# First blocks of batches 4 to 7: four turns in a row in score banks, two batches' scores in one burst, and the ban as a mask on VectorE

## Chip, cores and metric

The kernel runs on one core of one Trainium2 chip. The metric is the device time of an execution in microseconds (us). A core has TensorE (PE, with its weight loads shown as PEld), VectorE (DVE), ScalarE (ACT), GpSimd (POOL) and SyncE (SP, which here only issues transfers).

## What is computed

The reference is an attention with a forgetting gate, followed by a feed-forward layer on all 4608 rows:

```python
# q, k, v: 8 batches x 8 heads x 576 x 64; f: 8 x 8 x 576
scores = (1 / 8) * q @ k^T
cum    = cumsum(log(clip(f, 1e-4, 1)))
scores = where(causal, -1e9, scores + cum[:, :, :, None] - cum[:, :, None, :])
attn   = softmax(scores)
x      = (attn @ v) as 4608 rows of 512
h      = x @ w_in                      # 512 -> 2048
out    = (h * sigmoid(h)) @ w_out      # 2048 -> 512
```

The kernel takes the decay out of the softmax: v and a column of ones are multiplied by a weight per key, and the sums that come out in that column divide the rest.

## The kernel before

The 576 rows of a sequence are split into a first block of 128 rows, three more of 128, and a tail of 64. The **first blocks** of all eight batches are done ahead of the main loop, each with all eight heads at once. The **main loop** runs over 32 pairs of heads (n = 0 to 31), four pairs to a batch, and does the other rows. The **feed-forward** layer is work without order of its own: `m1_chunk` (lines 560 to 583) makes 128 of the 2048 hidden features for one group of rows (PE into a bank `hp`, tanh on ACT into `th`, the gate on DVE into `gt`), and `m2_part` (594 to 626) a quarter of an output tile `po`, which ACT copies and POOL stores. `fill` (698) puts such chunks between the attention's steps, by a budget in us at assumed costs, and `least` chunks in any case. So the order on each engine is fixed when the program is built; every engine runs its own list from front to back and waits for semaphores.

A first block of batch b has these steps:
- `load_qk0` (128): POOL issues the loads of q and k, as bf16, into a tile `qkb`.
- `turn0(b, i)` (277): 16 matmuls of 64x64 turn q (i = 0) or k (i = 1) into a bank `tp`; ACT copies q to `qT0` (a cast), DVE copies k to `kT0`.
- `ban0` (297): two matmuls of 512 columns put -30000 above the diagonal into a score tile, ahead of the scores. Or `mask0` (333): DVE multiplies the exponentials by a triangle of ones.
- `scores0` (309): 8 matmuls into a score tile `sc` of two banks, and one exp of 1024 columns on ACT.
- `out0` (349): 8 matmuls with the weighted v (`convert_v0`, 339, on POOL), then a reciprocal and a product on DVE into `xq`.
- `back0` (382): 4 transposes on PE into a bank `tx`, copied by ACT into the rows `x` that the feed-forward layer reads.

PSUM has eight banks: two score tiles of two banks each (pool `psc`, also for `out0`), and four single banks (pool `pbig`, tag `big`) that `tp`, `hp`, `po` and `tx` share.

Batches 0 to 3 form group 0 of the feed-forward's rows (512 wide), batches 4 and 5 group 1, 6 and 7 group 2 (256 wide each), and the main loop's rows groups 3 and on (384 wide, the tails 256). The change is in `two_more` (805), which does the first blocks of batches 4 and 5, and of 6 and 7, between chunks of the feed-forward layer: for 4 and 5 only first-layer chunks of group 0 are ready; from line 830 on the second layer is allowed too (`open2`). A group's chunks may start when `ready` has it.

In the main loop `scores(n, c)` (444) needs q and k of pair n turned: POOL casts them (`cast_qk`, 394), SP issues a transposing transfer into `qkT`, of which there are three (`transposes`, 423), SP also issues all loads, and POOL, in one list, casts, weights v (`convert_v`, 409) and issues the stores of finished output tiles.

Of the kernel before, what the change touches and what calls it, by code (L numbers as in the profile page):

```python
# [10 lines left out]
FP32 = mybir.dt.float32  # L11
BF16 = mybir.dt.bfloat16
P = 128
# [5 lines left out]
def kernel(  # L19
# [17 lines left out]
    NP = H // 2  # L37
    SM = 512
# [9 lines left out]
    RUN = 8  # L48
    NRUN = P // RUN
# [18 lines left out]
    psc = ctx.enter_context(tc.tile_pool(name="psc", bufs=2, space=bass.MemoryType.PSUM))  # L68
    pbig = ctx.enter_context(tc.tile_pool(name="pbig", bufs=4, space=bass.MemoryType.PSUM))
# [204 lines left out]
    qT0: dict[int, bass.AP] = {}  # L274
    u0: dict[int, bass.AP] = {}

    def turn0(b, i):
        src = qk0[b]
        if i == 0:
            qT0[b] = qktp.tile([P, NP, P], BF16, name="qT0", tag="qT0", bufs=2)  # L280
        dst, evac = ((qT0[b], nc.scalar.copy), (kT0[b], nc.vector.tensor_copy))[i]
        tp = pbig.tile([P, NP, NRUN, RUN], FP32, name="tp", tag="big")
        for c in range(RUN):
            for j in range(2):
                nc.tensor.matmul(
                    tp[j * D : (j + 1) * D, :, :, c].rearrange("p a r -> p (a r)"),
                    lhsT=src[:, i, c * D : (c + 1) * D],
                    rhs=sel[:, j, :],
                    start=True,
                    stop=True,  # L290
                )
        evac(
            out=dst[:, :, :].rearrange("p a t -> p (a t)"),
            in_=tp[:, :, :, :].rearrange("p a r c -> p (a r c)"),
        )

    def ban0(b):
        sc = psc.tile([P, 2, NP, P], FP32, name="sc", tag="sc")
        for i in range(2):
            nc.tensor.matmul(  # L300
                sc[:, i, :, :].rearrange("p a t -> p (a t)"),
                lhsT=ident_bf[:, :],
                rhs=ban[:, :, :].rearrange("p a t -> p (a t)"),
                start=True,
                stop=False,
            )
        return sc

    def scores0(b, sc=None):
        t = qT0.pop(b)  # L310
        fresh = sc is None
        u = upool.tile([P, 2, NP, P], BF16, name="u", tag="u")
        u0[b] = u
        if fresh:
            sc = psc.tile([P, 2, NP, P], FP32, name="sc", tag="sc")
        for p in range(NP):
            for i in range(2):
                r = slice(i * D, (i + 1) * D)
                nc.tensor.matmul(
                    sc[:, i, p, :],  # L320
                    lhsT=kT0[b][r, p, :],
                    rhs=t[r, p, :],
                    start=fresh,
                    stop=fresh or p == NP - 1,
                )
        nc.scalar.activation(
            out=u[:, :, :, :].rearrange("p i a t -> p (i a t)"),
            in_=sc[:, :, :, :].rearrange("p i a t -> p (i a t)"),
            func=ACT.Exp,
            scale=scale,  # L330
        )

    def mask0(b):
        x = u0[b][:, :, :, :].rearrange("p i a t -> p (i a) t")
        nc.vector.tensor_tensor(
            out=x, in0=x, in1=tri[:, None, :].to_broadcast([P, H, P]), op=ALU.mult
        )
# [11 lines left out]
    def out0(b, step_=2, apart=False):  # L349
        if apart:  # L350
            dns = [pbig.tile([P, 1, 4, D + 1], FP32, name="dn1", tag="big") for _ in range(2)]
        else:
            dn = psc.tile([P, 2, 4, P], FP32, name="dn0", tag="sc")
            dns = [dn[:, g : g + step_, :, :] for g in range(0, 2, step_)]
        k = 2 // len(dns)
        u = u0.pop(b)
        for h in range(H):
            p, i = h // 4 * 2 + h % 2, h // 2 % 2
            nc.tensor.matmul(
                dns[h // 4 // k][:, h // 4 % k, h % 4, 0 : D + 1],  # L360
                lhsT=u[:, i, p, :],
                rhs=v0[b][:, h, :],
                start=True,
                stop=True,
            )
        rec = recp.tile([P, 2, 4], FP32, name="rec0", tag="rec0")
        if not apart:
            nc.vector.reciprocal(out=rec[:, :, :], in_=dn[:, :, :, D])
        xq = xqp.tile([P, H, D], BF16, name="xq", tag="xq")
        for g, part in enumerate(dns):  # L370
            r = rec[:, g * k : (g + 1) * k, :]
            if apart:
                nc.vector.reciprocal(out=r, in_=part[:, :, :, D])
            nc.vector.tensor_tensor(
                out=xq[:, 4 * k * g : 4 * k * (g + 1), :].rearrange("p (g j) d -> p g j d", j=4),
                in0=part[:, :, :, 0:D],
                in1=r[:, :, :, None].to_broadcast([P, k, 4, D]),
                op=ALU.mult,
            )
        xqs[b] = xq  # L380
# [275 lines left out]
    def step(force=0):  # L656

        a, c = at["m1"], at["m2"]
        want = wanted(a, c)
        if not want:  # L660
            return None
        g1 = M1[a][0] if a < len(M1) else NG
        g2 = M2[c][0] if c < len(M2) else NG
        can1 = g1 in ready and not (M1[a][1] == 0 and g1 > g2 + 1)
        can2 = open2["w"] and c < len(M2) and g2 < g1
        kind = force if (force == 1 and can1) or (force == 2 and can2) else want
        if kind == 1:
            if M1[a][1] == 0:
                begin[g1] = (0, c)
            m1_chunk(g1, M1[a][1])  # L670
            at["m1"] += 1
            t = 4 * (GW[g1] / 2.4 + 2.5)
        else:
            m2_part(*M2[c])
            at["m2"] += 1
            t = 4 * (DM / 2.4 + 2.5)
        return t
# [6 lines left out]
    def plan(us_):  # L684

        a, c, kinds = at["m1"], at["m2"], []
        while us_ > 0:
            k = wanted(a, c)
            if not k:
                break  # L690
            kinds.append(k)
            if k == 1 and M1[a][1] == 0:
                begin[M1[a][0]] = (0, c)
            us_ -= (4 * (GW[M1[a][0]] / 2.4 + 2.5) if k == 1 else 4 * (DM / 2.4 + 2.5)) / 1000
            a, c = a + (k == 1), c + (k == 2)
        return kinds

    def fill(us_, least=0, ends=(0, 0)):

        left = us_ + at["left"]  # L700
        kinds = plan(left)
        kinds += [0] * (least - len(kinds))
        if any(ends) and kinds:
            if 2 not in kinds:
                kinds[0] = 2
            n1, n2 = len(kinds) - kinds.count(2), kinds.count(2)
            e0 = 1 if ends[0] else 0
            e1 = 1 if ends[1] and n2 > e0 else 0
            inner = n2 - e0 - e1
            n = n1 + inner  # L710
            mid = [2 if (x + 1) * inner // n > x * inner // n else 1 for x in range(n)]
            if inner and mid[-1] == 2 and e1 and not e0:
                mid = mid[::-1]
            kinds = [2] * e0 + mid + [2] * e1
        for k in kinds:
            t = step(k)
            if t is None:
                at["left"] = 0.0
                return
            left -= t / 1000  # L720
        at["left"] = left
# [3 lines left out]
    on_act, on_dve = nc.scalar.copy, nc.vector.tensor_copy  # L725
    weights_scan()
    turn0(0, 0)
    keep_warm(1)
    turn0(0, 1)
    nc.vector.tensor_copy(out=wexp[:, S : S + ST], in_=wexp[:, SM:S])  # L730
    bans = [ban0(0), ban0(1)]
# [4 lines left out]
    convert_v0(0)  # L736
    load_w_in(0)
    turn0(1, 0)
    turn0(1, 1)
    turn0(2, 0)  # L740
# [61 lines left out]
    for c in range(NM):  # L802
        convert_v(0, c)

    def two_more(b, banned):
        for x in range(2):
            turn0(b + x, 0)
            turn0(b + x, 1)
            fill(0.6, 1)
        for x in range(2):  # L810
            if banned:
                scores0(b + x, ban0(b + x))
            else:
                scores0(b + x)
                mask0(b + x)
            fill(0.6 if x == 0 else 2.0 if banned else 2.8, 1 if x == 0 else 2)
        out0(b)
        fill(0.6, 1)
        out0(b + 1)
        fill(0.8, 2)  # L820
        back0(b, on_act)
        fill(0.6, 1)
        back0(b + 1, on_act)
        fill(0.6, 1)

    fill(5.0)
    two_more(4, True)
    ready.add(1)
    fill(5.0)
    open2["w"] = True  # L830
    begin[M1[at["m1"]][0]] = (M1[at["m1"]][1], at["m2"])
    fill(6.0)
    two_more(6, False)
    ready.add(2)
    fill(3.2)

# [37 lines left out]
    for m in range(NQ):  # L874
# [5 lines left out]
        if m > 0:  # L880
            back(m - 1)
            if m % 2 == 0:
                b = m // 2 - 1
# [56 lines left out]
```

## Time and profile before

| what | us |
|---|---|
| executions: median of 3 (lowest, highest) | 343.55 (343.11, 345.07) |
| span of the profiled execution; its time isn't listed apart | 342.2 |
| PE busy | 334.3 |
| ACT, DVE, POOL busy | 216.8, 180.5, 130.0 |
| `two_more` for batches 4 and 5 | 23.4 to 36.3 |
| `two_more` for batches 6 and 7 | 46.6 to about 59.7 |
| first scores of the main loop | 61.1 |

The span reaches from the first to the last instruction that the profiler shows; the executions' times are some 1.35 us longer than it. "Busy" is the time in which an engine has an instruction in work; matmuls overlap, so a busy PE may still step slower than it could, and the distance from start to start tells more than the length of one. In a list by time each row has start, length, engine, line, operation, output and inputs, shape and count; a bracket gives the idle time ahead of it and what ended it. An operation such as `128*64 128x64` is a matmul with weights of 128 rows by 64 columns.

### The profile page before, as it was taken

How to read it: one execution, taken by the hardware profiler on the slowest of the kernel's cores; microseconds unless marked ns; L12 is line 12 of the kernel's file. 1: busy time of each engine (PE TensorE's matmuls, PEld its weight loads, DVE VectorE, ACT ScalarE, POOL GpSimd, SP SyncE). 2: the span in 40 equal slices, each digit the busy share in tenths (PEclk: the TensorE clock that was granted, in tenths of full speed). 3: DMA queues.
4: the chain of work that ended last, by engine and by line, in shares of the span. 5: the costliest groups of instructions: out<-in, count | busy, mean ns of one | idle time of the engine just before them, and what ended most of it. 6: DMA issues, size and time to landing. Idle time of an engine off the chain costs nothing.

```text
span 342.2 us, 8881 instructions
## 1 busy us (share of the span) xinstructions
PE 334.3 (98%) x3560; PEld 198.6 (58%) x3560; DVE 180.5 (53%) x387; ACT 216.8 (63%) x401; POOL 130.0 (38%) x227
## 2 busy tenths in 40 slices
PE   7999999999999999999999999999999999999995
PEld 3645655567656556566465666656656565555654
DVE  4665736357647547357445563655746364444330
ACT  5857645877687676857759677595685944454431
POOL 8895317732618307327325422612830000001011
PEclk9999999999999999999999999999999999999999
DMA  8999999999699889999999789989994010001012
GB/s 154 185 184 221 192 192 155 233 207 190 142 172 205 188 177 168 180 210 156 174 188 188 171 156 202 169 170 165 165 186 101 22 42 33 31 32 61 33 53 72
DMA packets 142457, 50.67 MB, mean 148 GB/s; under 512 B 133328, under 2 KB 139728, under 8 KB 142416
## 3 DMA queue, kind: packets, MB, share of 16 engines
q1 hardware_dynamic: 132400, 32.93, 56.7%
q0 software_dynamic: 9856, 17.04, 21.5%
q8 instruction: 28, 0.46, 0.6%
q10 hardware_dynamic: 160, 0.13, 0.1%
q14 instruction: 13, 0.11, 0.1%
HBM read 36.85 MB, written 9.44 MB: 135 GB/s over the span
## 4 chain that ended last, share of the span: by engine, by line
PE 66%; DMA 14%; SPq 9%; POOL 6%; issue 3%; ACT 0%; POOLq 0%
PE po L612 29%; PE hp L567 25%; DMA vf<-in_v_dram 6%; PE sc L459 5%; SPq L158 5%; PE dn L506 4%; DMA w_out_bf<-in_moe_w_out_dram 3%; PE dn L515 2%; SPq L427 2%; DMA qkT<-qkb 2%; POOL qkb L399 1%; DMA qkb<-in_k_dram 1%; SPq L168 1%; SPq L179 1%; DMA qf<-in_q_dram 1%
## 5 line engine op out<-in xcount | busy, mean ns | idle before, releaser
L576 DVE SCALAR_TENSOR_TENSOR gt<-th,hp 128x384 bf16<-128x384 bf16 (+2 forms) x208 | 105.8, 522 | 119.0 <-ACT th L575 115.5
L575 ACT ACTIVATE th<-hp 128x384 bf16<-128x384 f32 (+2 forms) x208 | 95.2, 478 | 84.3 <-PE hp L567 82.0
L612 PE MATMUL po<-w_out_bf,gt 128*128 128x512 bf16 (+1 forms) x592 | 145.3, 374 | 0.0
L567 PE MATMUL hp<-x,w_in_bf 128*128 128x384 bf16 (+2 forms) x704 | 128.1, 321 | 0.2
L567 PEld LDWEIGHTS <-w_in_bf 128*128 128x128 bf16 x832 | 79.9, 98 | 56.5 <-issue 0.7
L463 ACT ACTIVATE u<-sc 128x1024 bf16<-128x1024 f32 (+1 forms) x96 | 75.3, 822 | 9.5 <-PE sc L459 9.5
L612 PEld LDWEIGHTS <-gt 128*128 128x128 bf16 x592 | 53.3, 98 | 47.9 <-issue 2.5
L591 POOL DMA_DIRECT2D out_dram<-osb x38 | 21.0, 552 | 93.7 <-ACT osb L622 66.7
L413 POOL TENSOR_TENSOR vp<-vf,w_bf 128x520 bf16<-128x520 f32 (+1 forms) x32 | 34.4, 1078 | 41.0 <-DMA vf<-in_v_dram 35.1
L622 ACT ACTIVATE osb<-po 128x512 f32<-128x512 f32 (+1 forms) x37 | 22.1, 597 | 18.9 <-PE po L612 18.9
L399 POOL CAST qkb<-qf 128x384 bf16<-128x384 f32 x32 | 16.7, 521 | 41.9 <-DMA qf<-in_q_dram 41.2
L459 PE MATMUL sc<-qkT 64*128 64x128 bf16 (+1 forms) x640 | 26.9, 207 | 0.9 <-DMA qkT<-qkb 0.8
L459 PEld LDWEIGHTS <-qkT 64*128 64x128 bf16 x640 | 18.4, 94 | 12.5 <-issue 10.2
L467 ACT ACTIVATE ut<-sc 128x640 bf16<-128x640 f32 x32 | 23.3, 729 | 0.0
L476 DVE TENSOR_TENSOR u<-u,tri 128x768 bf16<-128x768 bf16 x32 | 22.1, 690 | 1.2 <-ACT u L463 1.2
L399 POOL CAST qkb<-kf 128x384 bf16<-128x384 f32 x32 | 17.7, 554 | 13.0 <-DMA kf<-in_k_dram 12.8
L506 PEld LDWEIGHTS <-u 128*128 128x128 bf16 x576 | 20.8, 98 | 2.5
L506 PE MATMUL dn<-vp,u 128*128 128x65 bf16 x384 | 21.8, 194 | 0.0
L524 DVE TENSOR_TENSOR xr<-dn,rec 128x448 bf16<-128x448 f32 x32 | 20.0, 624 | 1.1
L506 PE MATMUL dn<-v,u 128*128 128x65 bf16 x192 | 19.8, 194 | 0.0
L482 DVE TENSOR_TENSOR ut<-ut,trit 128x128 bf16<-128x128 bf16 x32 | 11.2, 351 | 15.6 <-ACT ut L467 15.6
L567 PE MATMUL hp<-xt,w_in_bf 128*128 128x256 bf16 x128 | 17.7, 273 | 0.0
(68 smaller groups left out, 203.0 us busy)
## 6 DMA issues: line engine op xcount, KB each, us to landing
out_dram<-osb POOLq DMA_DIRECT2D x32, 256.0 KB, 3.3
vf<-in_v_dram SPq DMA_DIRECT2D x26, 256.0 KB, 4.7
qf<-in_q_dram SPq DMA_DIRECT2D x64, 96.0 KB, 2.9
kf<-in_k_dram SPq DMA_DIRECT2D x64, 96.0 KB, 3.1
w_in_bf<-in_moe_w_in_dram POOLq DMA_DIRECT2D x4, 512.0 KB, 6.9
w_out_bf<-in_moe_w_out_dram POOLq DMA_DIRECT2D x4, 512.0 KB, 9.6
vf<-in_v_dram POOLq DMA_DIRECT2D x6, 256.0 KB, 10.3
qkb<-in_q_dram POOLq DMA_DIRECT2D x8, 128.0 KB, 5.1
```

The source lines that it names most:

```text
L399: nc.gpsimd.tensor_copy(out=t2[:, c0 : c0 + NR, :].rearrange("p c x -> p (c x)"), in_=t[:, :, :, :].rearrange("p c h d -> p (c h d)"),)
L413: nc.gpsimd.tensor_tensor(out=vbf[b][r, c, :, :], in0=vst[b][c][r, :, :], in1=w_bf[r, c + 1, b * H : (b + 1) * H, None].to_broadcast([n, H ...
L459: nc.tensor.matmul(sc[:, i, o : o + q1 - q0], lhsT=kt, rhs=t[r, q0:q1], start=True, stop=True)
L463: nc.scalar.activation(out=u[:, :, c * SM : c * SM + w], in_=sc[:, :, 0:w], func=ACT.Exp, scale=scale)
L467: nc.scalar.activation(out=ut[:, :, 0:3:2, :].rearrange("p k i t -> p i k t"), in_=sc[:, :, T0 : T0 + (NM + 1) * ST].rearrange("p i (k t) ...
L476: nc.vector.tensor_tensor(out=x, in0=x, in1=tri[:, None, None, :].to_broadcast([P, 2, NR, P]), op=ALU.mult)
L506: nc.tensor.matmul(dn[:, i * NR + c - 1, :], lhsT=u[:, i, o : o + P], rhs=vals(kb, i), start=(kb == 0), stop=(kb == c),)
L567: nc.tensor.matmul(hp[:, :], lhsT=w_in_bf[:, cc, fc * P : (fc + 1) * P], rhs=xcols(g, cc), start=(cc == 0), stop=(cc == NCC - 1),)
L575: nc.scalar.activation(out=th[:, :], in_=hp[:, :], func=ACT.Tanh, scale=0.5)
L576: nc.vector.scalar_tensor_tensor(out=gt[:, fc, :], in0=th[:, :], scalar=1.0, in1=hp[:, :], op0=ALU.add, op1=ALU.mult,)
L612: nc.tensor.matmul(po[:, :], lhsT=gt[:, fc, tb * P : (tb + 1) * P], rhs=w_out_bf[:, fc, m0:m1], start=(fc == 0), stop=(fc == NFC - 1),)
L622: nc.scalar.activation(out=osb[:, :], in_=po[:, :], func=ACT.Copy, scale=0.5)
```

## The change

In `two_more` the four turns of two batches come one after the other, with no chunks between them, each batch's two turns in the two banks of one score tile. The scores of both batches follow together. All four batches get the mask on DVE; the ban on PE is dropped for batches 4 and 5 (it stays for 0 to 3). The chunks between are redistributed, with budgets of 1.4 and 3.4 us in place of 0.6, 0.6, 0.6 and 2.0 (or 2.8).

```diff
-    def turn0(b, i):
+    def turn0(b, i, pair=None):
...
-        tp = pbig.tile([P, NP, NRUN, RUN], FP32, name="tp", tag="big")
+        if pair is None:
+            tp = pbig.tile([P, NP, NRUN, RUN], FP32, name="tp", tag="big")
+        else:
+            tp = pair[:, i, :].rearrange("p (a r c) -> p a r c", a=NP, c=RUN)
...
-    def two_more(b, banned):
+    def two_more(b):
         for x in range(2):
-            turn0(b + x, 0)
-            turn0(b + x, 1)
-            fill(0.6, 1)
-        for x in range(2):
-            if banned:
-                scores0(b + x, ban0(b + x))
-            else:
-                scores0(b + x)
-                mask0(b + x)
-            fill(0.6 if x == 0 else 2.0 if banned else 2.8, 1 if x == 0 else 2)
+            pair = psc.tile([P, 2, SM], FP32, name="tq", tag="sc")
+            turn0(b + x, 0, pair)
+            turn0(b + x, 1, pair)
+        fill(1.4, 2)
+        scores0(b)
+        scores0(b + 1)
+        mask0(b)
+        mask0(b + 1)
+        fill(3.4, 3)
         out0(b)
         fill(0.6, 1)
         out0(b + 1)
...
     fill(5.0)
-    two_more(4, True)
+    two_more(4)
...
-    two_more(6, False)
+    two_more(6)
```

## Prediction

> **What bounds the kernel now.** I read the page first, then what PE waited for, then PE's order of time from 20 to 112 us, then ACT, DVE and POOL in the same stretches, then the chain that ended last.
>
> ```profile
> span 342.2 us, 8881 instructions
> PE 334.3 (98%) x3560; PEld 198.6 (58%) x3560; DVE 180.5 (53%) x387; ACT 216.8 (63%) x401; POOL 130.0 (38%) x227
> ```
>
> PE has work in 98% of the span, so the time is PE's work plus its few waits. The waits are found in PE's order of time (start, length, engine, line, what, idle before):
>
> ```profile
> 73.70 0.28 PE L459 MATMUL sc<-qkT 64*128 64x64 bf16 x8
> 74.38 0.40 PE L459 MATMUL sc<-qkT 64*128 64x128 bf16 x8 [0.40 <-DMA qkT<-qkb]
> ...
> 111.07 0.28 PE L459 MATMUL sc<-qkT 64*128 64x64 bf16 x8
> 111.78 0.40 PE L459 MATMUL sc<-qkT 64*128 64x128 bf16 x8 [0.43 <-DMA qkT<-qkb]
> ```
>
> Eight such matmuls give way to the next group after about 0.12 us (0.28 less the last one's tail of some 0.17), so 74.38 comes 0.56 us late and 111.78 0.60 us late: the transposed q and k of head pairs 3 and 9 land too late. The chain that ended last says the same. Up to 111.78 it holds transfers, SP and POOL, and from there PE alone:
>
> ```profile
> 107.88 3.86 DMA qkT<-qkb
> ...
> 111.78 0.40 PE sc L459 x8
> ```
>
> So until 112 us an earlier PE meets a transfer, and after it every us of PE counts.
>
> **What goes.** PE around the first blocks of batches 4 and 5, and of 6:
>
> ```profile
> 24.45 1.04 PE L567 MATMUL hp<-x,w_in_bf 128*128 128x512 bf16 x4
> 25.42 1.08 PE L285 MATMUL tp<-sel,qkb 128*64 128x64 bf16 x32
> 26.43 1.04 PE L567 MATMUL hp<-x,w_in_bf 128*128 128x512 bf16 x4
> 27.31 0.59 PE L300 MATMUL sc<-ban,ident_bf 128*128 128x512 bf16 x2
> 27.83 0.40 PE L319 MATMUL sc<-qT,kT 64*128 64x128 bf16 x8
> 28.16 1.04 PE L567 MATMUL hp<-x,w_in_bf 128*128 128x512 bf16 x4
> ...
> 46.60 1.08 PE L285 MATMUL tp<-sel,qkb 128*64 128x64 bf16 x32
> 47.62 0.61 PE L567 MATMUL hp<-x,w_in_bf 128*128 128x256 bf16 x4
> ```
>
> Steps from start to start are the cost here, since lengths overlap. Four 512-wide matmuls step 0.88 us before the ban (26.43 to 27.31) and 0.97 before a turn (24.45 to 25.42): going into the narrow shapes costs 0.09.
> - Bans of batches 4 and 5: 27.31 to 27.83 is 0.52 us, less the 0.09 of entering the scores, which stays: 0.43. Twice: **-0.86**.
> - Scores of two batches in one burst: two bursts of 0.33 (27.83 to 28.16) and an entry of 0.09 each become one entry and 0.55 (the eight more matmuls step 0.22; leaving is paid once). -0.2 in each of two places: **-0.4**.
>
> **What the four turns in a row cost.** The built program of the changed kernel carries a wait that the diff doesn't show: the first matmul of every turn of k waits for ACT's copy of q out of the same score tile, though that copy reads the tile's other bank. Before, the turns had tiles of their own. No row of before has this wait, but its parts do:
>
> ```profile
> 47.28 0.58 ACT L292 CAST qT<-tp 128x512 bf16<-128x512 f32 x1 [1.86 <-PE tp L285]
> ```
>
> ACT starts 0.68 us after the turn pair does (46.60) and needs 0.58; with some 0.04 for the signal the turn of k starts at 1.30 instead of 0.45. The next batch's turn of q has another tile and follows at once (1.75), its turn of k starts at 3.05, and the filler at 3.62. Before, the two bursts took 1.02 each (46.60 to 47.62) and a second entry of 0.09, in all 2.13. So +1.49 a burst, in two bursts: **+2.98**. What is queued behind the wait on PE is everything, for no filler stands within the burst. Bounds: no wait at all gives -0.2 a burst; a copy that starts a whole 0.6 us ACT row later, twice a burst, gives +2.7. I take 1.49, whose parts are rows.
>
> The skill bears on this: the Trainium skill, "PSUM — Partial Sum Buffer", section "PSUM bank collisions raise a hardware error", asks for semaphores by bank and quadrant, and says that different banks don't collide. By that rule the wait isn't needed, and a program guarded so would come out as my first rival; but here the program's own wait decides.
>
> **What the masks and the long burst cost.** For batches 4 and 5 both exps and both masks now stand ahead of the filler's tanh on ACT and gate on DVE. Rows:
>
> ```profile
> 51.64 1.14 DVE L335 TENSOR_TENSOR u<-u,tri 128x1024 bf16<-128x1024 bf16 x1 [1.66 <-ACT u L326]
> 53.04 1.20 DVE L335 TENSOR_TENSOR u<-u,tri 128x1024 bf16<-128x1024 bf16 x1
> ...
> 35.35 2.00 DVE L576 SCALAR_TENSOR_TENSOR gt<-th,hp 128x512 bf16<-128x512 bf16 x3
> ```
>
> With the filler's start after the turns as zero: scores are issued by 2.38, exps end at 3.47 and 4.40 (1.02 each), masks at 4.7 and 5.8, and gates follow at 0.60 each (2.00 for three is 0.69 and 0.65 a step). Four filler banks are full at 5.84; the fifth chunk, after out0, is due at 6.10 and gets its bank at 6.39 (0.29). The DVE then has two divisions of 0.85 among the gates: the chunk after the first way back is due at 9.46 and starts at 9.63 (0.17). The last way back is issued by 10.72, and here group 0 is used up: the chunk after it is group 1's first, which reads what ACT copies out of that way back. ACT is at a tanh until 11.2, then copies until 11.77:
>
> ```profile
> 36.52 0.58 ACT L390 COPY x<-tx 128x512 bf16<-128x512 bf16 x1
> ```
>
> Before, a 512-wide chunk of group 0 stood over this copy; in the changed order none is left. PE waits 1.09. Together 1.55, against 0.45 lost before in this stretch (four 512-wide matmuls take 1.10 from 34.96 to 36.06 instead of 0.88, and the 4 of 512 and 24 of 256 columns from 36.28 to 40.02 take 3.74 where 4 x 0.216 + 24 x 0.108 are 3.46): **+1.1**, between 0 (DVE had been early) and 1.6. For batches 6 and 7 the masks were there already, and the filler is half as heavy on DVE: nothing.
>
> POOL converts v beside these masks:
>
> ```profile
> 30.02 2.11 POOL L340 TENSOR_TENSOR v<-vf,w_bf 128x520 bf16<-128x520 f32 x2 [3.98 <-DMA vf<-in_v_dram]
> ...
> 51.19 2.51 POOL L340 TENSOR_TENSOR v<-vf,w_bf 128x520 bf16<-128x520 f32 x2
> ```
>
> Two conversions took 2.11 us alone and 2.51 beside masks. In the new order they end by 32.5, and out0 of batch 4 is due at about 33: hidden.
>
> **What moves.** Counting the matmuls in both orders, the changed one has 8 more 256-wide and 8 more 512-wide filler matmuls ahead of the main loop's first scores (8 x 0.108 + 8 x 0.216 = 2.6 us); the total is the same. With -0.86 -0.4 +2.98 +1.1 = +2.8 PE reaches the first scores 5.4 us later. Then the tiles of pairs 3 and 9 have landed: **-1.16**, and the score bank that came 0.27 late at 63.2 is free: **-0.2**. SP's and POOL's orders keep loads and transposes as they were. On POOL a fourth store now stands ahead of pair 3's casts and one that PE releases at about 73.4 ahead of pair 4's (70.8 before); a transpose also waits for scores three pairs back. I estimate 1 to 2 us for these on the transfers, less than PE's own delay there. Later the filler ahead shrinks to +0.9 (pair 13) and -0.65 (pair 17): pair 13's tile landed at 139.2, 0.6 ahead of its scores, pair 17's 1.2 ahead, so a PE that is 1.5 later than before on balance still finds them, by under 2 us.
>
> **Sum.** -0.86 -0.4 +2.98 +1.1 -1.16 -0.2 = +1.46 us on a span of 342.2. The median of the runs is 343.55, 1.35 above the span; I leave this as it is: **345.0**.
>
> **Rivals.**
> 1. The turns don't wait (the copy is done when the matmul asks): bursts -0.4 instead of +2.98, so PE loses 0.6, arrives at pairs 13 and 17 earlier than they land, and gives back some 0.6 of the 1.36: 343.55 -0.6 -1.36 +0.6 = 342.2. For it: the banks differ. Against it: the built wait. 0.08.
> 2. The backlog costs nothing (DVE caught up during the turn stalls): 345.0 - 1.1 = 343.9. 0.15.
> 3. The transfers slide with PE: POOL's store ahead of pair 4's casts holds them until PE gets there, and every later load and transpose is behind them on SP, so the two waits at pairs 3 and 9 return elsewhere (9, 13 or 17): 345.0 + 1.36 = 346.4, slower. It decides once the transfers slip by over 2 us at pair 13. For it: transfers set the chain up to 112 us. Against it: between those slots SP waits for POOL some us, which is slack. 0.25.
>
> The forecast has 0.52. The range takes in rival 3 and most of rival 2: 343.6 to 346.8. About what this measurement can tell from no change is 0.5%, 1.72 us: 345.27 and 341.83. Slower by more: rival 3 and some three tenths of the forecast, 0.40; faster by more: 0.04; within: 0.56.
>
> **What would show it.** In the changed profile: a gap of about 0.85 us ahead of each of four turns of k, released by ACT's cast; a gap near 1 us after the last way back of batch 5, released by the copy; no wait for qkT at pairs 3 and 9; PE's busy time down by 1 to 2 us while its gaps grow. It is wrong if the turns run without gaps, if pairs 9, 13 or 17 wait for transfers, or if new waits on score banks appear in the main loop.

## The result, and the profile after

The changed kernel takes 347.02 us (median of 6 runs, 346.81 to 348.22), the kernel before 344.41 in the same comparison (6 runs, 343.11 to 345.74). The ratio is 1.0072, 95% interval 1.0043 to 1.0101: slower by 1.5 to 3.5 us. The forecast was +1.46 us and 345.0. Of the 2.02 us that it missed by, 0.86 is the base, whose median went from 343.55 with three runs to 344.41 with six; the other 1.16 is the change itself, +2.61 by the medians. In the runs here an execution's time lies 1.73 to 1.95 us above its own span, not 1.35, so the span of 342.2 that the sum started from stands for about 344.0 (an estimate from these).

The profiled execution of the changed kernel ran 347.17 us with a span of 345.4. The page's head and its line of engines:

```profile
span 345.4 us, 8880 instructions
...
PE 334.5 (97%) x3556; PEld 199.3 (58%) x3556; DVE 180.9 (52%) x389; ACT 217.0 (63%) x401; POOL 129.1 (37%) x227
```

PE has as much busy time as before in a span that is 3.2 us longer. So the loss is idle time of PE. What PE waited for (us in total, times, longest), from the view of waits:

```profile
PE tq L288 <- ACT qT L295: 2.7, 4, 0.7
...
PE dn L509 <- DVE gt L579: 0.9, 2, 0.5
PE hp L570 <- ACT x L393: 0.9, 1, 0.9
...
PE tx L551 <- DVE xr L527: 0.4, 1, 0.4
```

Before, from batch 4 on, PE's order of time showed two waits of this kind alone, 0.40 and 0.43 us for transfers. The first and the third line were forecast. The second and the fourth were not, and the second decides this case. PE in order of time in the first blocks of batches 4 and 5 (start, length, line, what, idle before):

```profile
23.05 0.64 PE L288 MATMUL tq<-sel,qkb 128*64 128x64 bf16 x16
24.36 1.08 PE L288 MATMUL tq<-sel,qkb 128*64 128x64 bf16 x32 [0.68 <-ACT qT L295]
26.12 0.64 PE L288 MATMUL tq<-sel,qkb 128*64 128x64 bf16 x16 [0.67 <-ACT qT L295]
26.69 0.60 PE L570 MATMUL hp<-x,w_in_bf 128*128 128x512 bf16 x2
...
38.39 0.81 PE L570 MATMUL hp<-x,w_in_bf 128*128 128x256 bf16 x6 [0.86 <-ACT x L393]
```

A group of 16 is one turn. After the turn of q at 23.05 PE stands still until ScalarE has copied q; the 32 at 24.36 are the turn of k and the next batch's turn of q, and then PE stands again. ScalarE's side of it:

```profile
23.73 0.58 ACT L295 CAST qT<-tq 128x512 bf16<-128x512 f32 x1
25.49 0.58 ACT L295 CAST qT<-tq 128x512 bf16<-128x512 f32 x1 [1.17 <-PE tq L288]
```

The copies end at 24.31 and 26.07, and the turns of k start 0.05 us later each.

A gap in brackets counts from the modelled end of the last matmul. In what follows a step is called **late** by what it takes from start to start beyond the same pair of shapes where nothing waits; the gap of 0.68 is 0.90 late, that of 0.86 is 1.02. From the first turn of batch 4 PE needs 37.64 us to the main loop's first scores before and 42.90 after (61.07 - 23.43, 65.95 - 23.05). I count from that turn, because in the profiled executions of this study it comes anywhere from 22.9 to 25.4 us, with the same code ahead of it in all of them.

The first scores of pairs 3 and 9 stand without a gap behind the 64-wide ones of the pair before them now, eight and eight in one row of 16. Pair 17's do not:

```profile
78.53 0.50 PE L462 MATMUL sc<-qkT 64*128 64x64 bf16 x16
...
116.17 0.50 PE L462 MATMUL sc<-qkT 64*128 64x64 bf16 x16
...
169.74 0.40 PE L462 MATMUL sc<-qkT 64*128 64x128 bf16 x8 [0.33 <-DMA qkT<-qkb]
```

Instead PE is late at places that had no wait before: 0.42 at 75.8 (transposes behind VectorE's division), 0.57, 0.30 and 0.62 at 83.9, 110.9 and 190.7, each at the first matmul of a pair's second attend, and 0.49 at pair 17. PE, VectorE and GpSimd around the first of these second attends, from the timeline:

```profile
82.99 1.05 POOL L416 TENSOR_TENSOR vp<-vf,w_bf 128x520 bf16<-128x520 f32 x1 [6.30 <-DMA vf<-in_v_dram]
...
83.17 0.94 DVE L485 TENSOR_TENSOR ut<-ut,trit 128x128 bf16<-128x128 bf16 x1 [0.76 <-ACT ut L470]
...
84.04 0.74 DVE L579 SCALAR_TENSOR_TENSOR gt<-th,hp 128x256 bf16<-128x256 bf16 x2
84.50 0.19 PE L509 MATMUL dn<-v,u 128*128 128x65 bf16 x1 [0.41 <-DVE gt L579]
```

Read from the bottom: the attend needs a bank of the pool "big", which the first of the two gates at 84.04 frees; that gate stands on VectorE behind the tail mask of the same pair; and the tail mask takes 0.94 us. The same mask ten us earlier:

```profile
73.08 0.22 DVE L485 TENSOR_TENSOR ut<-ut,trit 128x128 bf16<-128x128 bf16 x1 [0.74 <-ACT ut L470]
```

What is different at 83 is POOL's line: GpSimd converts v at the time. The theory from here on, **A**: the four gaps are ScalarE's copies; the gap at 38.39 is the order of chunks; and the time that the prediction thought won in the main loop goes into masks that meet conversions. The rivals are named with each run.

### The profile page after: what moved, and what is told of

It is laid out like the page before. It is cut to its first block, busy times and chain, and to the rows that moved or that the text cites. A ratio compares the mean times of both kernels' runs of the same rounds, so it can differ in the third digit from the quotient of the medians.

```text
span 345.4 us, 8880 instructions
## 1 busy us (share of the span) xinstructions
PE 334.5 (97%) x3556; PEld 199.3 (58%) x3556; DVE 180.9 (52%) x389; ACT 217.0 (63%) x401; POOL 129.1 (37%) x227
## 4 chain that ended last, share of the span: by engine, by line
PE 77%; ACT 6%; DMA 5%; SPq 4%; DVE 3%; issue 3%; POOL 1%; POOLq 0%; ACTq 0%
PE po L615 32%; PE hp L570 29%; PE sc L462 5%; PE dn L509 4%; DMA vf<-in_v_dram 3%; ACT th L578 2%; PE dn L518 2%; SPq L158 2%; DMA qkT<-qkb 2%; DVE gt L579 2%; PE wm L232 1%; ACT u L466 1%; PE tq L288 1%; ACT ut L470 1%; DVE ut L485 1%
## 5 line engine op out<-in xcount | busy, mean ns | idle before, releaser
L570 PE MATMUL hp<-x,w_in_bf 128*128 128x384 bf16 (+2 forms) x704 | 126.4, 321 | 1.0 <-ACT x L393 0.9
L416 POOL TENSOR_TENSOR vp<-vf,w_bf 128x520 bf16<-128x520 f32 (+1 forms) x32 | 35.7, 1114 | 42.5 <-DMA vf<-in_v_dram 31.4
L479 DVE TENSOR_TENSOR u<-u,tri 128x768 bf16<-128x768 bf16 x32 | 20.7, 648 | 3.1 <-ACT u L466 3.1
L402 POOL CAST qkb<-kf 128x384 bf16<-128x384 f32 x32 | 16.6, 519 | 9.5 <-DMA kf<-in_k_dram 9.5
```

The lines of the kernel that those rows point to most:

```text
L402: nc.gpsimd.tensor_copy(out=t2[:, c0 : c0 + NR, :].rearrange("p c x -> p (c x)"), in_=t[:, :, :, :].rearrange("p c h d -> p (c h d)"),)
L416: nc.gpsimd.tensor_tensor(out=vbf[b][r, c, :, :], in0=vst[b][c][r, :, :], in1=w_bf[r, c + 1, b * H : (b + 1) * H, None].to_broadcast([n, H ...
L570: nc.tensor.matmul(hp[:, :], lhsT=w_in_bf[:, cc, fc * P : (fc + 1) * P], rhs=xcols(g, cc), start=(cc == 0), stop=(cc == NCC - 1),)
```

## Experiments: the first blocks

All ratios are to the kernel before, from runs on the same chip.

**The copies after both turns.** Nothing else is changed in the changed kernel; `turn0` hands its copy back in place of issuing it.

```diff
...
-            turn0(b + x, 0, pair)
-            turn0(b + x, 1, pair)
+            copies = [turn0(b + x, i, pair) for i in range(2)]
+            for copy in copies:
+                copy()
```

> The changed kernel, but each batch's two copies (q on ACT, k on DVE) are issued after both turns, so that no turn of k waits for ACT. Theory A (the four gaps of 0.90 us ahead of the turns of k cost their full length): 3.6 us less than the changed kernel, about 0.99 us under the kernel before, with four gaps gone in PE's order and the other waits of the changed kernel unchanged. Rival B (the transfers set the pace of the main loop, and a PE that is early gives the time back there): under 1.5 us gained on the changed kernel, the rest as new waits for qkT.

344.12 us, ratio 1.0002 (0.9979 to 1.0025). The turns of a burst run as one row:

```profile
23.37 1.98 PE L288 MATMUL tq<-sel,qkb 128*64 128x64 bf16 x64
25.28 1.04 PE L575 MATMUL hp<-x,w_in_bf 128*128 128x512 bf16 x4
```

From the first turn to the main scores 39.31 us instead of 42.90: 3.59 less, four times 0.90. So the gaps are the wait for the copy and nothing else, and in size they are about the whole of the change's loss. That the kernel comes out level with the kernel before and not under it is a first sign that the main loop doesn't pay back what it should: PE is late there by 0.42, 0.18, 0.38, 0.32 and 0.77.

**Turns in single banks of the other pool**, four in a row still; the rest as in the changed kernel.

```diff
-            pair = psc.tile([P, 2, SM], FP32, name="tq", tag="sc")
-            turn0(b + x, 0, pair)
-            turn0(b + x, 1, pair)
+            turn0(b + x, 0)
+            turn0(b + x, 1)
```

> The changed kernel with one part undone: each turn goes to a single bank of the other pool as in the kernel before, four in a row still; bursts, masks and fills are the changed kernel's. Theory A (PE waits for ScalarE's copy of q only because k's turn shares the tile): the four gaps of 0.9 us go, as with the copies moved; the gap of about 0.9 us after the last way back stays; first main scores at 62.5 to 63; time 343.8 to 344.4. Theory B (the wait comes from four turns in a row, whatever banks they use): gaps of 0.5 us and more stay and the time is 345.5 to 347.

344.38 us, ratio 0.9991 (0.9966 to 1.0015); 39.85 us to the main scores. The four gaps are gone with the order unchanged, and the gap after the last way back stays at 1.02 late. It is the shared tile that makes the turn of k wait, not the row of four.

**The same four in a row, alone in the kernel before.**

```diff
             turn0(b + x, 0)
             turn0(b + x, 1)
-            fill(0.6, 1)
+        fill(1.2, 2)
```

> The kernel before, with the four turns of two batches in a row in the four single banks, and the two fillers after them; nothing else changed. Theory A (two entries into the narrow shape saved, 0.2 us each): no gap in the bursts, 64 matmuls in 1.95 us, the main loop reached 0.4 us earlier, and the end within 0.4 us of before. Rival B (four turns in a row wait for something else, a copy or a bank, as in the changed kernel): gaps of 0.5 us or more in or behind the bursts, and 1 us or more slower.

344.06 us, ratio 0.9992 (0.9970 to 1.0014), no gap in the bursts, 37.30 us to the main scores (37.64 before). A burst without the shared tile is free and saves some 0.3 us there. In the main loop of this run, whose chunks stand in the order of before, one attend is 0.70 late at 159.7, behind a mask that took 1.07 us beside conversions of v. The kernel before has no such wait there, so the moment counts too, and not the order of chunks alone.

**The mask alone, in the kernel before.**

```diff
-            if banned:
-                scores0(b + x, ban0(b + x))
-            else:
-                scores0(b + x)
-                mask0(b + x)
+            scores0(b + x)
+            mask0(b + x)
```

> The kernel before, with the mask on DVE in place of the ban on PE for batches 4 and 5 and all else as it was. Theory A (four ban matmuls are 0.86 us of PE; the two masks fit beside the filler between): PE reaches the main loop 0.86 us earlier, waits as much longer at pairs 3 and 9, and ends within 0.5 us of the kernel before. Rival B (DVE can't take the masks): gaps for filler banks in the stretch from 27 to 40 us of over 0.9 us, and the main loop is reached no earlier.

344.22 us, ratio 1.0007 (0.9986 to 1.0027). PE has two bans less, 0.86 us, and nothing is won. Against what theory A expected, the profiled execution (345.69 us, above the median) comes to the main scores no earlier, 37.75 us after the first turn: the outputs of batches 5, 6 and 7 (`out0`) are 0.30, 0.36 and 0.16 late, each behind GpSimd's conversion of v. The one for batch 5 takes 1.44 us beside the masks, 1.05 in the kernel before. Chunks around the masks run as before, so theory B's late banks didn't come either. At pair 3, whose tile landed at 75.3 instead of 74.3, PE is then 1.73 late instead of 0.56.

**The ban kept, in the changed kernel.**

```diff
-        scores0(b)
-        scores0(b + 1)
-        mask0(b)
-        mask0(b + 1)
+        for x in range(2):
+            scores0(b + x, ban0(b + x) if b == 4 else None)
+        if b != 4:
+            mask0(b)
+            mask0(b + 1)
```

> The changed kernel, but batches 4 and 5 keep the ban as PE writes instead of the mask on VectorE. Theory A (the stall after the last way back comes from the order of chunks, not from the masks): the gap at about 38 us stays at 0.7 to 0.9 us, the four gaps ahead of the turns of k stay at 0.7 busy-based, and PE has some 0.86 us of bans more, so that the first main scores come 0.7 to 0.9 later and the time is 347.5 to 348. Theory B (VectorE's masks make the backlog that stalls PE): the gap shrinks to under 0.3 us and the time is 346.5 to 347.1, no more than the changed kernel's.

348.23 us, ratio 1.0121 (1.0086 to 1.0155), 43.65 us to the main scores: 0.75 more than with the masks. The gap after the last way back is there without any mask, 0.87 late. So it comes from the order: no chunk of group 0 is left to stand over ScalarE's copy.

**One chunk of group 0 kept for that place**, with the copies after both turns.

```diff
-        fill(3.4, 3)
+        fill(2.5 if b == 4 else 3.4, 3)
```

> The changed kernel with two edits in the first blocks: the two copies of a batch's turns are asked for after both turns (as in the run before), and the fill after the score burst of batches 4 and 5 is cut from 3.4 to 2.5, so that one chunk of group 0 is left for the place after the last way back. Theory A (the gap of 0.86 us ahead of the first chunk of group 1 is PE waiting for ScalarE's copy, only because no chunk of group 0 is left): that gap goes, the first scores of the main loop come 0.8 to 0.9 us earlier than with the copies moved alone, and the time falls from 344.1 to about 343.2. Theory B (time won before the main loop is given back there, because waits come back when the order of chunks shifts): the gap goes and the time stays at 343.8 to 344.4, with the waits after 60 us larger by the amount won.

345.56 us, ratio 1.0039 (1.0017 to 1.0062): slower than with the copies alone. The gap shrinks to 0.26, but the outputs of batches 4, 5 and 7 are 0.39, 0.34 and 0.38 late, behind GpSimd's conversions of v:

```profile
30.42 2.51 POOL L348 TENSOR_TENSOR v<-vf,w_bf 128x520 bf16<-128x520 f32 x2 [3.08 <-DMA vf<-in_v_dram]
30.54 1.48 DVE L343 TENSOR_TENSOR u<-u,tri 128x1024 bf16<-128x1024 bf16 x1 [0.23 <-ACT u L334]
...
31.52 0.42 PE L367 MATMUL dn<-v,u 128*128 128x65 bf16 x8 [0.23 <-POOL v L348]
```

The masks of the first blocks meet conversions too: the mask takes 1.48 us here and 0.69 alone, and the second conversion 1.50 instead of 1.05. In the changed kernel these conversions are hidden, as the prediction had it: they end at 31.77 and the first output starts at 32.54, since PE comes there later by its waits in the turns. The main loop is late by 0.32 at 66.4 (a score tile, just behind ScalarE's exp), 0.67 at 132.8 and 0.86 at 188.6 (second attends). The order of chunks has changed, and it meets other waits. From the first turn on the profiled execution is 1.0 us longer than with the copies alone, and its steps that are over 0.1 late add up to 4.5 us against 3.5, so the waits account for it.

## Experiments: the main loop

**Only the order shifted.** The kernel before, with a longer fill as the last thing ahead of the main loop, so that its chunks stand as in the changed kernel.

```diff
-    fill(3.2)
+    fill(5.8)
```

> The kernel before, with the last filler budget ahead of the main loop 5.8 instead of 3.2 us: four chunks (2 of 256 columns, 2 of 512) more before the first scores, and the main loop's order of chunks as in the changed kernel. Theory A (the prediction's): the waits at pairs 3 and 9 and the late score bank vanish and nothing replaces them: 1.2 to 1.6 us under the kernel before. Rival B (the new order of chunks brings waits of its own, for DVE ahead of the attend steps and for a late transfer at pair 17): within 0.7 us of the kernel before or slower, with over 1 us of new gaps in the main loop.

344.53 us, ratio 1.0004 (0.9986 to 1.0022). The waits at pairs 3 and 9 vanish, 1.16 us, and PE is late by 0.39, 0.76, 0.70 and 0.64 elsewhere, the last three at attends. With none of the change's parts in the kernel the exchange is the same, so it comes from the shift alone. One of these places in the timeline:

```profile
106.58 2.49 POOL L413 TENSOR_TENSOR vp<-vf,w_bf 128x520 bf16<-128x520 f32 x2
...
106.97 1.05 DVE L482 TENSOR_TENSOR ut<-ut,trit 128x128 bf16<-128x128 bf16 x1
...
108.54 0.19 PE L506 MATMUL dn<-v,u 128*128 128x65 bf16 x1 [0.59 <-DVE gt L576]
```

**The tail mask behind the gates**, in the changed kernel.

```diff
-        mask_tail(n + 1)
         slot(piece, 1, 0)
+        mask_tail(n + 1)
         attend(n)
```

> The changed kernel with one call moved in the main loop: the tail mask of a pair's second half is issued after the third slot's chunks and not ahead of them, so that VectorE does the gates of these chunks first. Theory A (the new waits ahead of the second attend of a pair are for a bank that the gate frees, and the gate stands behind a mask that takes 0.9 to 1.0 us beside GpSimd's conversions): the three waits of 0.57, 0.30 and 0.62 us go, about 1.2 to 1.5 us less, time 345.5 to 345.8. Theory B (the bank is late for another reason, or the mask then holds up the attend itself): waits of the same size stand at the attends or in their last matmuls, and the time stays at 346.7 to 347.3.

347.51 us, ratio 1.0096 (1.0064 to 1.0128): no gain. The attends start in time, or nearly (0.18, 0.11, 0.11 late), but their last matmuls wait for the mask (0.52, 0.51, 0.26 and 0.22 late):

```profile
74.89 0.46 DVE L485 TENSOR_TENSOR ut<-ut,trit 128x128 bf16<-128x128 bf16 x1
...
75.41 0.20 PE L518 MATMUL dn<-vp,ut 128*128 128x65 bf16 x1 [0.36 <-DVE ut L485]
```

This is the second clause of theory B: a late mask holds either the gate or the attend. **All three edits together** (copies, chunk and mask) carry that over:

> All three edits together on the changed kernel: copies after both turns, one chunk of group 0 kept, tail mask after the third slot's chunks. If each wait has the cause that theory A gives, the gains add: 347.0 - 2.9 - 0.9 - 1.3 = about 342 us, under the kernel before by 2. If waits are only traded for each other (theory B), no less than 343.5.

346.62 us, ratio 1.0071 (1.0046 to 1.0096). The gaps at the turns and after the last way back are gone, but three outputs of the first blocks are 0.28 to 0.34 late, and one attend alone loses 1.62 at 106.5. The gains do not add.

**The conversions moved** behind a batch's last attends, in the changed kernel, with the copies moved as well, and in the kernel before.

```diff
-        if p >= 2:
-            for c in range(2 * (p - 2), 2 * (p - 1)) if b > 0 else range(NM * (p - 2)):
-                convert_v(b + 1, c)
...
         attend(n + 1)
+        if n % NP == NP - 2 and n // NP + 1 < B:
+            for c in range(NM):
+                convert_v(n // NP + 1, c)
```

> The changed kernel with GpSimd's four conversions of the next batch's v moved, in the main loop alone, from the slots of a batch's last two pairs to behind the last pair's attends, so that no conversion of about 1.05 us runs beside VectorE's tail masks; nothing else is changed on PE, VectorE or ScalarE. Theory A (the new waits at the second attend come from masks that take 0.6 to 1.0 us beside these conversions, and 0.22 alone): the masks ahead of these attends fall to 0.2 to 0.4 us, the waits of 0.57, 0.30 and 0.62 us go, and the time is 345.4 to 345.9. Theory B (the masks are slow or the gates late for another reason, or the wait only moves on, to the casts and transfers that now stand behind the conversions): 346.7 or more, with waits for a transfer or at other attends of 1 us and more in all.

> The changed kernel with the copies after both turns (344.1 before) and the conversions moved as well. Its waits at attends were 0.18, 0.38 and 0.77 us. Theory A: they go, time about 342.8 to 343.2. Theory B: 344 or more.

> The kernel before with the conversions moved and nothing else. Its waits at pairs 3 and 9 (0.56 and 0.60 us) are for transfers, and no wait at an attend is over 0.11 us. Theory A: nothing to gain, 344.2 to 344.8; casts that stand behind the conversions may add up to 0.5 at a transfer. Theory B (the conversions burden the loop as a whole): under 343.5.

354.96 us (1.0292, 1.0258 to 1.0327), 351.97 (1.0216, 1.0170 to 1.0261) and 352.47 (1.0222, 1.0186 to 1.0258). The edit missed its aim, and by that showed the mechanism: GpSimd came to the conversions late, behind a store that waited for ScalarE, and did four in a row, where masks stood again. From the changed kernel with the conversions moved:

```profile
188.16 0.54 POOL L594 DMA_DIRECT2D out_dram<-osb  x1 [2.87 <-ACT osb L625]
...
188.72 4.55 POOL L416 TENSOR_TENSOR vp<-vf,w_bf 128x520 bf16<-128x520 f32 x4
...
189.22 2.67 DVE L485 TENSOR_TENSOR ut<-ut,trit 128x128 bf16<-128x128 bf16 x1
...
192.27 1.07 DVE L485 TENSOR_TENSOR ut<-ut,trit 128x128 bf16<-128x128 bf16 x1
...
193.27 1.01 DVE L579 SCALAR_TENSOR_TENSOR gt<-th,hp 128x384 bf16<-128x384 bf16 x2
...
193.86 0.19 PE L509 MATMUL dn<-v,u 128*128 128x65 bf16 x1 [1.57 <-DVE gt L579]
```

A mask of 0.22 us takes 2.67 beside four conversions, and PE idles 1.57. Even the kernel before, whose profile has no such wait, gets them (1.73 and 1.67 late at 163 and 195). The waits aren't the whole of these losses. In the profiles of these runs the granted clock of PE falls to 0.50 for 3.41 us around the end of such a wait, twice in the first run (from 194.1 and 255.6) and once in each of the others (249.3, 165.3), and 512-wide matmuls step 0.43 us there where they take 0.22 else. That is some 1.7 us each time, an estimate from the two steps. It didn't follow every such wait: behind the one at 195 in the last run the clock stayed at 1.00.

**Without the conversions** from batch 2 on, in the changed kernel; batches 2 to 7 attend with the v of batches 0 and 1. That leaves out 24 of the 32 conversions, where the expectation says 28.

```diff
     def convert_v(b, c):
         vbf[b] = vps[b % 2]
+        if b > 1:
+            return
```

> The changed kernel without GpSimd's conversions of v from batch 2 on (28 of the 32 in the main loop are left out; batches 2 to 7 attend with the v of batches 0 and 1, so the output differs). PE, VectorE and ScalarE do all that they did. Theory A (VectorE's tail mask, 0.22 us alone, lasts 0.6 to 1.0 beside a conversion, the gates behind it come late, and PE waits at the second attend): all masks from 95 us on take 0.22 to 0.35 us; the waits of 0.30 us at 110.9 and 0.62 at 190.7 go, that of 0.57 at 83.9, beside the conversions of batch 1 that are kept, stays; GpSimd's casts come earlier too, so the wait of 0.49 for a transfer at 169.2 may go. Time 345.5 to 346.3. Theory B (the gates are late for PE whatever GpSimd does): the waits at 110.9 and 190.7 stay at 0.3 and 0.6 and the time is 346.6 or more.

346.22 us, ratio 1.0051 (1.0032 to 1.0070). All masks but two take 0.22 to 0.23 us (0.43 and 0.29 the others). The view of waits has the gaps of the first blocks and nothing at an attend any more:

```profile
PE tq L288 <- ACT qT L295: 2.7, 4, 0.7
...
PE hp L572 <- ACT x L393: 0.9, 1, 0.9
PE tx L553 <- DVE xr L529: 0.4, 1, 0.4
```

The attends are late by 0.18 and 0.11 at most, and pair 17's transfer is there in time. The wait at 83.9, whose conversions were kept, went too, against what was expected: its mask took 0.43 this time. **Without the tail masks**, the other side of the meeting:

> The changed kernel without VectorE's 32 tail masks of the main loop (the output of the tail queries differs). Theory A: all three waits at second attends (0.57, 0.30, 0.62 us) go, the gaps of the first blocks stay, main-loop waits over 0.1 us add up to 1.0 instead of 2.6, time 345.2 to 345.8. Theory B (the gate itself, not what stands ahead of it on VectorE, is too late): the waits shrink by less than half, time 346.5 or more.

346.11 us, ratio 1.0054 (1.0035 to 1.0073), the attends late by 0.18 and 0.11 at most: the waits go, and the time is 0.3 to 0.9 us above what was expected.

**Without the conversions and with the copies after both turns:**

> The changed kernel with the copies after both turns (ratio 1.000 to before) and without the conversions of v from batch 2 on (output differs). Theory A: its waits of 0.18, 0.38 and 0.77 us at second attends go, the gap of 0.87 after the last way back and 0.42 at pair 4 stay; 1.0 to 1.6 us under the run with the copies moved alone, so about 342.6 to 343.2, ratio 0.994 to 0.997. Theory B: ratio 0.998 or more.

342.69 us, ratio 0.9940 (0.9918 to 0.9961). The changed order with nothing to meet on VectorE and GpSimd is faster than the kernel before; but GpSimd has 24 conversions less to do here, and what that alone is worth isn't shown. **The kernel before without the tail masks**, as a control:

> The kernel before without VectorE's 32 tail masks (output of the tail queries differs). Theory A (in the order of before no attend waits for a gate behind a mask; its waits of 0.56 and 0.60 us at pairs 3 and 9 are for transfers): both waits stay, ratio 0.997 to 1.001. Theory B (the masks cost the main loop time in any order): ratio 0.996 or less.

343.68 us, ratio 0.9970 (0.9950 to 0.9989). Here the transfers at pairs 3 and 9 are 1.08 and 0.81 late, more than with the masks. The ratio lies on the edge between the two theories, so the masks may cost the old order a little as well.

**The meeting taken away with all work done.** The conversions of batches 2 to 7 go to VectorE's own queue, in the changed kernel with the copies after both turns, and in the kernel before.

```diff
-            for c in range(2 * (p - 2), 2 * (p - 1)) if b > 0 else range(NM * (p - 2)):
+            for c in range(0) if b > 0 else range(NM * (p - 2)):
...
+    def on_vector(n, *cs):
+        b = n // NP + 1
+        if n % NP == NP - 2 and 1 < b < B:
+            for c in cs:
+                convert_v(b, c, nc.vector)
...
         mask(n)
+        if m > 0:
+            on_vector(n - 2, 3)
...
+        on_vector(n, 0)
         mask_tail(n + 1)
...
         attend(n + 1)
+        on_vector(n, 1, 2)
```

> The changed kernel with the copies after both turns, and with the conversions of v of batches 2 to 7 (24 of them) done by VectorE itself in place of GpSimd: one ahead of the second tail mask of a batch's last two pairs, two behind their attends, one behind the first mask of the next two pairs. The work is whole. Theory A (waits at second attends come from masks that meet GpSimd's conversions; in one queue they cannot meet): masks at 0.22 to 0.5 us, the waits of 0.18, 0.38 and 0.77 go, time near the run without conversions, 342.6 to 343.4, ratio 0.994 to 0.997, under the kernel before. Theory B (a conversion of some 0.6 to 1.1 us on VectorE, an estimate from its 0.62 us for 448 elements, holds up gates as the slow masks did): waits of 0.5 us and more for gates, ratio 0.998 or more.

> The kernel before with the same conversions on VectorE. Theory A: its waits at pairs 3 and 9 are for transfers and stay; GpSimd's casts come earlier, so that the second may shrink; ratio 0.996 to 1.000. Theory B: new waits for gates, ratio 1.001 or more.

343.76 us, ratio 0.9973 (0.9940 to 1.0005), and 345.02, ratio 1.0014 (0.9986 to 1.0042). VectorE in the first of them:

```profile
185.54 0.55 DVE L484 TENSOR_TENSOR u<-u,tri 128x768 bf16<-128x768 bf16 x1
186.01 0.69 DVE L421 TENSOR_TENSOR vp<-vf,w_bf 128x520 bf16<-128x520 f32 x1
186.64 0.23 DVE L490 TENSOR_TENSOR ut<-ut,trit 128x128 bf16<-128x128 bf16 x1
187.02 1.02 DVE L584 SCALAR_TENSOR_TENSOR gt<-th,hp 128x384 bf16<-128x384 bf16 x2 [0.16 <-ACT th L583]
```

One conversion more in this queue, and the gates still come earlier than behind a mask that met GpSimd: the attends are late by 0.18 and 0.11 only, as in the run that left the conversions out. So it is the meeting and not the amount of work that made those attends late. But against the copies alone the time fell by 0.4 us by the medians (1.0 by the ratios), and without the conversions by 1.4 (2.1); in the kernel before, both waits for transfers vanish too, and the time does not fall. At pair 3 that isn't the edit's work, since no conversion ahead of it was moved: PE came to its first turn of batch 4 later in this profile, at 25.21 instead of 23.43. At pair 9 the tile landed earlier, at 110.6 instead of 111.7. Where these last tenths go stays open. No version that does all the work is faster than the kernel before by more than the measurement can tell; the changed kernel with the copies moved and the conversions on VectorE comes nearest to it, and is 3.3 us under the changed kernel (343.76 to 347.02, against bases 0.02 us apart).

## Why the prediction was off

- **Bans, -0.86**: held, about. With the ban put back PE arrives 0.75 later.
- **The scores in one burst, -0.4**: held. The burst takes 0.56 us (28.52 to 29.08), forecast 0.55.
- **The four turns, +2.98**: held. The burst takes 3.64 us from its first turn to the filler (23.05 to 26.69), forecast 3.62. Rival 1 is out: the wait is there, and both runs that take the shared tile's wait away bring 39.3 and 39.9 us to the main scores instead of 42.9.
- **Masks and long burst, +1.1**: held, nearly in full, so rival 2 is out. The gap after the last way back is 1.02 late (forecast 1.09) and is an effect of the order, as the prediction had it. The fifth chunk is 0.17 late (0.29), the chunk after the first way back 0.16 (0.17), and the last way back 0.08: 1.43 lost, forecast 1.55. The 0.45 that the prediction subtracts for the kernel before are 0.50 by its own two readings (0.22 and 0.28), so it is +0.93 measured.
- **The arrival at the main loop, +5.4**: 42.90 - 37.64 = +5.26. The terms above and the 2.6 us of filler done earlier add up to 5.3.
- **"Then the tiles of pairs 3 and 9 have landed: -1.16", and the score bank, -0.2**: both waits vanish. But the sum takes them as won, with nothing for what PE would meet in their place, and this is the step that failed. From the main scores to the end the profiled execution gains 281.17 - 279.44 = 1.73 us; 2.6 of it is filler done earlier, so the loop itself is 0.87 us slower, where -1.36 was forecast. Its late steps over 0.1 us are 1.73 before (0.27, 0.20, 0.56, 0.60, 0.11) and 2.68 after (0.42, 0.57, 0.30, 0.17, 0.49, 0.62, 0.11). The difference, 0.94, is about that of the loop. One execution scatters here: four other runs with the changed order of chunks take 279.10 to 279.45 for this stretch, a second one with the order of before (turns in own banks) 281.64. By all of these the loop is 0.1 to 0.9 us slower, and in none is the 1.36 won.
- **Pair 17**, which the prediction thought safe by under 2 us: its tile landed at 169.7 instead of 166.7 and is 0.49 late. Without GpSimd's conversions it is there in time.
- **Rival 3** gave the nearest time, 346.4, and that is luck: its condition didn't come. It had the transfers slide with PE, by over 2 us at pair 13; pair 9's tile landed at 112.0 after and 111.7 before, pair 13's at 139.6 and 139.3. Only pair 17's is late, as said. The rest of what takes the place of the old waits is VectorE.
- **A sign that didn't show**: PE's busy time was to fall by 1 to 2 us. It is 334.5 and was 334.3; from the first turn on alone it falls by 0.6 (314.0 to 313.4).

By the two profiled executions, counted from that turn, the change costs 5.26 - 1.73 = 3.53 us, more than the 2.61 of the medians. The sizes above carry an uncertainty of this order.

What I overlooked stood in the profile before. I looked for what PE would meet 5 us later on SP's and POOL's queues, that is among the transfers, and not on VectorE. Most of its 32 tail masks take 0.22 us, but nine of them overlap a conversion of v there, and five of these took 0.68 to 1.12; they lay where no attend was due. Two of the five, from the timeline of before:

```profile
243.80 2.51 POOL L413 TENSOR_TENSOR vp<-vf,w_bf 128x520 bf16<-128x520 f32 x2
243.81 1.12 DVE L482 TENSOR_TENSOR ut<-ut,trit 128x128 bf16<-128x128 bf16 x1
...
245.32 1.07 DVE L482 TENSOR_TENSOR ut<-ut,trit 128x128 bf16<-128x128 bf16 x1
```

I had even weighed POOL's side of such a meeting (2.11 and 2.51 us), and not VectorE's.

The Trainium skill, "SBUF — State Buffer", section "Who interferes with whom", says that a VectorE instruction with two inputs in SBUF contends with a GpSimd instruction that reads there. The tail mask and the conversion are of these kinds, and the runs agree: masks without a GpSimd instruction beside them take 0.22 to 0.23 us in both kernels, those beside conversions up to 1.12, and without the conversions 30 of 32 take 0.22 to 0.23.

## What to carry to other kernels

A wait that vanishes because the engine arrives later is not won: list, for the new arrival, every wait that has little slack, on every queue, and in particular what stands on VectorE ahead of the instruction that frees a bank. Where two-input VectorE work can fall beside GpSimd's reads, take its long duration for the sum and not its usual one. And a copy out of one half of a tile makes a writer of the other half wait if the program guards the tile as a whole; issue both writers first, or give them tiles of their own.

## What was not expected of the hardware

- The 128x128 tail mask on VectorE takes 0.22 us alone. Beside GpSimd's conversions it took up to 1.12 in the two kernels, 2.67 beside four in a row, and 3.17 at most (the changed kernel with the conversions moved). So it isn't held for one conversion of 1.05 us only, but can be for more than two.
- The same conversion takes 1.05 us on GpSimd and 0.69 on VectorE, and 0.89 to 1.00 on VectorE at a few places.
- A mean hides this: the 32 masks of the changed kernel average 0.35 us.
